# Attention, a dense MoE layer and a routed MoE layer in one program: GpSimd held back at one place, a third PSUM bank for one product, and routing's matmul groups at new places

## The chip, the core and the metric

The program runs on one core of a Trainium2 chip. The core has five engines that run their own instruction streams and wait for one another by semaphores: PE (TensorE, matmuls), DVE (VectorE), ACT (ScalarE), POOL (GpSimd) and SP (SyncE, which here only issues transfers). The metric is the device time of one execution in microseconds; lower is better. A time of this kernel is taken as the median of a few executions, and from one program to the next about 0.2% (1.9 us) can be told from no change.

## What is computed

Three layers follow one another. The tokens are 4 batches of 768, with 8 heads of 64, so x is 3072 x 512 between the layers.

```python
# 1: attention with a window of 128 and 4 sink positions
scores = (q @ k.T) / 8                       # per batch and head
keep   = (pos < 4) | ((0 <= rel) & (rel < 128))
a = softmax(where(keep, scores, -1e9));  x = a @ v
# 2: a dense layer with three input products
h = max(max(x @ w1, x @ w2), x @ w3)         # 512 -> 768
x = h @ w_out                                # 768 -> 512
# 3: routing with a limited capacity, 8 experts of 384 tokens
logits = x @ w_gate
# all (token, expert) pairs are taken in falling order of their logit; a pair is
# skipped if the token is assigned or the expert is full
out[tokens of e] = relu(x[tokens of e] @ w1[e]) @ w2[e]
```

## The kernel before

**Products in three parts.** A matrix product that needs float32 is made from float32r parts: each operand is split into a rounded part (`h`, ACT copies it) and the rest (`l`, a subtraction on DVE or POOL), and PE adds hh, hl and lh. So nearly every tile in the trace has an `h` and an `l`, and for every split there is one ACT instruction and one subtraction.

**Attention** (`class Attn`) works in 32 units: a unit is one batch, one half of the sequence (`hf`) and one pair of heads (`p`); four units make a group, and `n` counts units in the order in which they are loaded. `load` issues the unit's transfers, `prep` splits k (`kh`, the subtraction is L106), q (`qs` by ACT in L107, the rest `ql` in L108) and v (`vsp`, rounded part in L119 on ACT, the rest in L120 on POOL), `score` makes the scores (PE L138, or L140 and L141 for a split unit; tile `ps`) and copies them under the mask into T (`T_w`, `T_x`; in the first units parts of the storage `woh`, `wol` serve as tiles), `soft` does maximum, exponential and sum, with POOL multiplying by the reciprocal (L163), and `pv` transposes T on PE (the sinks' columns into the PSUM tile `pt`, the window's into `pp`, both L25), masks them into A (L179), and multiplies with v (PE L186, L188, L198, L199 into `po`). The first eight units and units 10 and 11 are native: PE takes q, k and v as float32, with no split. **Unit 8 is the first split unit, and unit 9 the second.**

**The dense layer** (`class Moe1`) loads its weights while attention's first units run: `single` puts 64-bit words together to one float32 tile (DVE L245 and L249, ACT L246, POOL L250 into `cA` or a part of `HL`), and `load_w` splits that into `w0`, `w1`, `w2` (ACT L229, POOL L231). There are 18 such words for the input weights, counted by `s.n`, and 6 for w_out. `group` makes the three input products of a group of 384 tokens, 12 matmuls per product (PE L305 into `mm`), and the maximum (ACT L307, DVE L308); it splits the result into `HL`. `x2` multiplies with w_out: 6 products of 18 matmuls each (PE L330), 260 columns wide with the gate's logits in them (n=260) for groups 0 to 4; ACT evicts each (L332, tile `xo`). Group 0 is written out and read back by `reload` (L347 to L350), since its weights are not there in time. Five x2 of this form stand between 175 and 440 us.

**The routed layer** (`class Route`, `class Moe2`). Routing finds one full expert after another: a `phase` counts by digits of the logits, six levels, each with 24 small matmuls (PE L432, tile `rc`), a comparison before it (DVE L427, `th`) and a digit after it (DVE L479 to L483, `met`), then a sum (L490) and ranks (L523, L524, L555). `expert` runs eight blocks f of 12 matmuls (L634) and 9 matmuls (L627), 168 in all, and splits the weights it loads (`wa`, `wb`; ACT L578, DVE L579) and the hidden values (ACT L637, DVE L638). While expert n runs, the routing of expert n+2 runs on DVE, and its groups of small matmuls are put between the expert's matmuls.

**What sets the order.** Attention and the dense layer lie in one block whose instructions a scheduler orders by a timeline of its own when the program is built (`schedule_with_timeline_sim=True`), under priorities, tile pools and the extra dependences that `follow` adds. PSUM has eight banks of 128 x 512 float32: two for `mm`, one each for `pt`, `pp` and `po`, three for `ps`. A pool with one buffer is used strictly in the order in which the program asks for it. Routing's groups are put behind given matmuls of the expert by `behind` and a list of places, one for each group: the six levels, the sum, the two ranks and the slots.

Of the kernel before, what the change touches and what calls it, by code (L numbers as in the profile page):

```python
# [19 lines left out]
FT=mybir.dt.float32; FR=mybir.dt.float32r; BF=mybir.dt.bfloat16; I32=mybir.dt.int32; U8=mybir.dt.uint8; U32=mybir.dt.uint32  # L20
AF=mybir.ActivationFunctionType; OP=mybir.AluOpType; AX=mybir.AxisListType
NEG=-8.0e9
def f32(ap): return ap.bitcast(FT)
# [3 lines left out]
def split(nc,hl,x):  # L27
    i=nc.scalar.activation(hl[0],x,AF.Copy)
    nc.vector.tensor_tensor(hl[1],x,f32(hl[0]),op=OP.subtract)
    return i  # L30

def follow(tc,i,j):
    tc.add_manual_dep(i.ins,j.ins.name,mybir.DependencyInfo(mybir.DependencyClass.NoSync,mybir.DependencyReason.DATA),reason="order on an engine")

class Attn:
    def __init__(s, tc, q,k,v,vs, keep, consts, pst, psp, pss, psv, work):
# [57 lines left out]
    def prep(s,u):  # L94
        nc=s.nc; w=s.w; nb=u['nb']; nat=u['nat']
        half=[(slice(64*h,64*h+64),slice(64-64*h,128-64*h)) for h in range(2)]
        if not nat:
            KK=[s.two(u,[128,4,132],FR,f"kh{h}") for h in range(2)]
            QS=[w.tile([128,384],FR,name=f"qs{h}",bufs=2) for h in range(2)]
            QL=s.ql[u['n']%len(s.ql)]  # L100
            fl=nb*132
            flat=lambda t: t.rearrange("p c j -> p (c j)")[:,:fl]
            for h,(a,o) in enumerate(half):
                k=flat(u['kn'])[a]
                nc.scalar.activation(flat(KK[h])[a],k,AF.Copy)
                nc.vector.tensor_tensor(flat(KK[h])[o],k,f32(flat(KK[h])[a]),op=OP.subtract)  # L106
                nc.scalar.activation(QS[h],u['qn'][h],AF.Copy)  # L107
                nc.vector.tensor_tensor(QL[h][a],u['qn'][h][a],f32(QS[h][a]),op=OP.subtract)  # L108
            u.update(KK=KK,QS=QS,QL=QL)
        VK=u['VK']=s.vk[u['n']%2]  # L110
        hi,lo=(bass.AP(tensor=VK.tensor,offset=VK.offset+o,ap=[[VK.ap[0][0],40],[st,2],[1,64]]) for o,st in (((0,64),(128,64)) if nat else ((0,192),(64,64))))
        nc.gpsimd.tensor_copy(hi,u['sv'])
        nc.gpsimd.tensor_tensor(lo,u['sv'],f32(hi),op=OP.subtract)
        if not nat:

            VS=u['VS']=w.tile([128,4,256],FR,name="vsp")
            hi=bass.AP(tensor=VS.tensor,offset=VS.offset,ap=[list(VS.ap[0]),[256,nb],[192,2],[1,64]])
            lo=bass.AP(tensor=VS.tensor,offset=VS.offset+64,ap=[list(VS.ap[0]),[256,nb],[64,2],[1,64]])
            nc.scalar.activation(hi,u['vn'][:,:nb],AF.Copy)  # L119
            nc.gpsimd.tensor_tensor(lo,u['vn'][:,:nb],f32(hi),op=OP.subtract)  # L120
    def score(s,u):
        nc=s.nc; w=s.w; hf=u['hf']
        if type(s.extra) is not Spare: T=s.two(u,[128,6,132],FT,"T",3)
# [3 lines left out]
        if hf==0:  # L127
            z=nc.gpsimd.memset(T[:,0:2,:],NEG)
            if u['n']==3: follow(s.tc,z,s.ev['s',1])
# [89 lines left out]

class Moe1:  # L220
    def __init__(s, tc, words,wgate, consts, wpool, main, conv, mm, pt, pss, ident):
        s.tc=tc; s.nc=tc.nc; s.mm=mm; s.pss=pss; s.main=main; s.conv=conv; s.ident=ident; s.consts=consts
        s.src=words; s.wgate=wgate
        s.W=[[wpool.tile([128,4,768],FR,name=f"w{i}{x}") for x in "hl"] for i in range(3)]
        s.WO=None; s.at=None; s.stage=None; s.HL=None; s.nx=0; s.second=None; s.n=0; s.loads=[]
        s.WG=main.tile([128,6,16],FR,name="wgt")
    def split(s,src,hi,lo):
        nc=s.nc
        z=nc.scalar.activation(hi,src,AF.Copy)  # L229
        if s.n==5 and s.WO is None: follow(s.tc,z,s.ev['l',4])  # L230
        nc.gpsimd.tensor_tensor(lo,src,f32(hi),op=OP.subtract)  # L231
    def single(s,src,ring=False):

        nc=s.nc
        if ring and s.stage is None: s.stage=s.main.tile([128,12,384],FT,name="HL").rearrange("p a b -> p (a b)").bitcast(I32)
        if ring: st=s.stage[:,s.n%4*1024:(s.n%4+1)*1024].rearrange("p (n t) -> p n t",t=2)
        else: st=s.conv.tile([128,512,2],I32,name="st",bufs=2)
        ld=nc.sync.dma_start(st.rearrange("p n t -> p (n t)"),src.bitcast(I32))
        if ring: s.loads.append(ld)
        else: s.tc.add_manual_dep(ld.ins,s.loads[-6].ins.name,mybir.DependencyInfo(mybir.DependencyClass.NoSync,mybir.DependencyReason.DATA),reason="order of loads")  # L240
        A=(s.mm.tile([128,512],FT,name="mm") if ring and s.n<3 else s.pss.tile([128,512],FT,name="ps")).bitcast(I32); C=st[:,:,0]
        if ring and s.n%3==2: R=s.stage[:,4096:4608]
        else: R=s.conv.tile([128,512],I32,name="cA",bufs=2)
        n=s.n; s.n+=1
        y=nc.vector.tensor_scalar(A,st[:,:,1],0x07ffffff,3,op0=OP.bitwise_and,op1=OP.logical_shift_left)  # L245
        z=nc.scalar.activation(C,st[:,:,0].bitcast(U32),AF.Copy,scale=2.0**-29)  # L246
        if n<4: follow(s.tc,z,s.ev['l',0] if n<2 else s.ev['e',1])
        if n<3: follow(s.tc,y,s.ev['m',1 if n<1 else 2])
        nc.vector.scalar_tensor_tensor(R,st[:,:,1],-0x40000000,A,op0=OP.bitwise_and,op1=OP.bitwise_or)  # L249
        nc.gpsimd.tensor_tensor(R,R,C,op=OP.add)  # L250
        return R.bitcast(FT)
    def pair(s,p):
        return tuple(s.main.tile([128,384],FR,name=f"x{x}{p}",bufs=1) for x in "hl")
# [33 lines left out]
    def group(s,xs,spill=None,pool=None,mid=None,between=None):  # L287
# [3 lines left out]
        for p in range(4):  # L291
            if type(xs[p]) is tuple: X.append(xs[p]); continue
            X.append(s.pair(p))
            with s.tc.high_priority(): split(nc,X[p],xs[p])
# [24 lines left out]
    def x2(s,H,t0,LG,x2d,n=260,pool=None,keep=None):  # L319

        nc=s.nc; main=s.main; mms=[]
        for t in range(3):
            o=pool.tile([128,512],FT,name="xq",bufs=4) if pool else s.room(t).tile([128,520],FT,name="xo",bufs=1)
            for u in range(2):
                c=slice(0,260) if n==260 else slice(4-4*u,260-4*u)
                ps=s.mm.tile([128,512],FT,name="mm")
                k=0
                for f in range(6):
                    for a,b in ((0,0),(0,1),(1,0)):
                        mms.append(nc.tensor.matmul(ps[:,:n],H[f][a][:,t*128:(t+1)*128],s.WO[b][:,f,u,c],start=(k==0),stop=(k==17))); k+=1  # L330
                with s.tc.high_priority():
                    nc.scalar.activation(o[:,u*n:(u+1)*n],ps[:,0:n],AF.Copy)  # L332
                    if keep is not None:
                        for d in (2*u,2*u+1):
                            h,l=keep(t,d); c=ps[:,(d-2*u)*128:(d-2*u)*128+128]
                            nc.scalar.activation(h,c,AF.Copy)
                            nc.vector.tensor_tensor(l,c,f32(h),op=OP.subtract)
            if n==260:
                o,e=s.row(o,0)
                nc.scalar.activation(LG[:,t0+t,:].rearrange("p (u e) -> p u e",u=2),e,AF.Copy)  # L340
            nc.scalar.dma_start(x2d[(t0+t)*128:(t0+t+1)*128,:],o)
        return mms
# [307 lines left out]
def attention_mixtures(tc,q,k,v,vs,words,wg,u1,u2,out,off=60,spread=(0,1,3,4),native=8,order='a0 a0 a0 a0 w a1 w a1 w a1 w a1 w w a2',order1='a2 o o o o o o a2 a2',back=1,at=(1,0),s1=300,s2=400,nring=6):  # L650
    nc=tc.nc
    PS=bass.MemoryType.PSUM
    with ExitStack() as ctx:
        P=lambda n,b,**kw: ctx.enter_context(tc.tile_pool(name=n,bufs=b,**kw))
        A_=lambda n,b,**kw: tc.alloc_tile_pool(name=n,bufs=b,**kw)
        consts=P("consts",1); main=P("main",1); dram=P("dram",1,space=bass.MemoryType.DRAM)
        wpool=A_("wpool",1,side="right"); ac=A_("ac",1); work=A_("work",2); conv=A_("conv",1,side="right")
        mm=P("mm",2,space=PS); pst=P("pst",1,space=PS)
# [62 lines left out]
        E=Moe2(tc,u1,u2,x2d,out,wp,act,main,mm,acc,pst,A.ident,nring,M.part)  # L721
        def step(n):
            e,t=r.phase(n>0) if n<7 else r.last()
            return r.slots(e,t)
        def fet(n):
            G.append([E.fetch(S[n][0],None if n else T7*128),S[n][1],S[n][0]])
        def trn(n):
            G[n][0]=E.turn(G[n][0],None if n else (keep,P7))
            G[n][1]=nc.sync.value_load(G[n][1][0:1,0:1],min_val=0,max_val=7)
        def behind(gs,mms,places):  # L730

            for ins,at in zip(gs,places):
                for i in ins:
                    tc.add_manual_dep(i.ins,mms[at].ins.name,mybir.DependencyInfo(mybir.DependencyClass.NoSync,mybir.DependencyReason.DATA),reason="order on TensorE")
# [22 lines left out]
        for n in range(8):  # L757
            r.groups=[]
            if n<6:
                with tc.high_priority(offset=s2): S.append(step(n+2)); fet(n+2)  # L760
            gs,r.groups=r.groups,[]
            E.expert(*G[n],mid=(lambda: trn(n+1)) if n<7 else None)
            if n<6: behind(gs,E.mms,(40,74,88,102,116,130,143,156,165,167) if n==0 else (20,47,64,81,98,115,131,145,156,160) if n<5 else (4,16))


_INS = ['q', 'k', 'v', 'vs', 'words', 'wg', 'u1', 'u2']
# [50 lines left out]
```

## Time and profile before

| what | us |
|---|---|
| median of three runs (lowest, highest) | 962.07 (961.85, 962.66) |
| the profiled execution, its own time | 963.42 |
| its span, first to last instruction | 961.6 |
| PE busy in the span | 927.3 (96%) |
| DVE busy | 705.2 (73%) |
| ACT busy | 487.7 (51%) |
| POOL busy | 257.1 (27%) |

The profiled execution is 1.35 us above the median, and 1.8 us of its time lie outside its span. Busy time of PE is the time in which a matmul is in flight; matmuls overlap, so a busy PE can still be one that issues below its rate. A wait is the idle time of an engine just before an instruction, and the releaser is the instruction whose end came last. Times in rows count from the span's start.

### The profile page before, as it was taken

The numbers are of one execution on the slowest core, as the hardware profiler recorded it, in microseconds if no ns is written. First come the engines' busy times: TensorE is split into PE (matmuls) and PEld (weight loads), VectorE is DVE, ScalarE is ACT, GpSimd is POOL, SyncE is SP. The second block draws the span as 40 slices with busy tenths as digits, with TensorE's granted clock in tenths as the row PEclk, the third lists the DMA queues.
The fourth block names the chain that finished last, engine by engine and source line by source line (L and its number), as shares of the span: only waits on it lengthen the run. The fifth ranks groups of instructions, "written<-read, shape, count | busy, mean of one in ns | idle before, by whom it ended". The sixth has DMA issues, their size and how long they took to land.

```text
span 961.6 us, 18493 instructions
## 1 busy us (share of the span) xinstructions
PE 927.3 (96%) x6552; PEld 850.4 (88%) x6552; DVE 705.2 (73%) x1867; ACT 487.7 (51%) x1329; POOL 257.1 (27%) x271
## 2 busy tenths in 40 slices
PE   5999899989999999999999999999999999999996
PEld 4688799979999999999999998888888888888895
DVE  7776787687887886778896445888989889874320
ACT  5366474687677675676674211334434434344431
POOL 4676536132321312211231000011103022054321
PEclk9999899999999999999999999999999999999999
DMA  7454321242123121122210002544345353454410
GB/s 233 137 191 144 105 93 64 81 145 68 52 63 94 41 85 57 44 79 85 81 57 1 1 1 88 192 145 132 111 154 176 103 169 119 151 194 156 142 66 33
DMA packets 54443, 99.35 MB, mean 103 GB/s; under 512 B 7792, under 2 KB 24688, under 8 KB 54352
## 3 DMA queue, kind: packets, MB, share of 16 engines
q1 hardware_dynamic: 44464, 75.90, 25.3%
q0 software_dynamic: 3840, 12.45, 3.7%
q10 hardware_dynamic: 6048, 9.83, 2.7%
q8 instruction: 51, 0.84, 0.4%
q14 instruction: 40, 0.33, 0.1%
HBM read 82.17 MB, written 16.12 MB: 102 GB/s over the span
## 4 chain that ended last, share of the span: by engine, by line
PE 82%; DVE 6%; issue 5%; ACT 3%; DMA 2%; POOL 1%; SPq 0%; POOLq 0%; ACTq 0%; DVEq 0%
PE mm L305 28%; PE mm L634 13%; PE acc L627 12%; PE mm L330 8%; PE po L198 3%; PE rc L432 3%; PE po L188 2%; PE pt L25 2%; PE ps L138 2%; PE pp L25 2%; PE ps L140 1%; PE ps L141 1%; PE acc L362 1%; PE po L199 1%; DMA qf<-in_q_dram 1%
## 5 line engine op out<-in xcount | busy, mean ns | idle before, releaser
L627 PE MATMUL acc<-wbh,HL 128*128 128x512 f32 x384 | 133.1, 401 | 0.1
L308 DVE TENSOR_TENSOR hm<-mm,hm 128x384 f32<-128x384 f32 x96 | 53.2, 554 | 50.7 <-PE mm L305 49.5
L330 PE MATMUL mm<-woh,HL 128*128 128x260 f32 (+1 forms) x432 | 86.0, 289 | 2.7 <-ACT xo L332 1.2
L627 PEld LDWEIGHTS acc<-wbh,HL 128*128 128x128 f32 x384 | 71.4, 188 | 12.6 <-ACT HL L637 0.4
L578 ACT ACTIVATE wah<-sa 128x512 fp32r<-128x512 f32 x64 | 40.5, 632 | 82.2 <-PE mm L634 69.3
L578 ACT ACTIVATE wbh<-sb 128x512 fp32r<-128x512 f32 x64 | 40.4, 631 | 72.8 <-PE acc L627 68.9
L627 PE MATMUL acc<-wbl,HL 128*128 128x512 f32 x192 | 76.5, 398 | 0.0
L646 POOL DMA_INDIRECT out_dram<-og,idx x24 | 29.3, 1221 | 168.7 <-ACT og L645 165.9
L330 PEld LDWEIGHTS mm<-woh,HL 128*128 128x128 f32 x432 | 68.4, 188 | 4.7 <-ACT xo L332 1.9
L634 PE MATMUL mm<-HL,wah 128*128 128x384 f32 x256 | 67.5, 341 | 0.0
L305 PE MATMUL mm<-xh,w2h 128*128 128x384 f32 x192 | 66.8, 348 | 0.2 <-ACT hm L307 0.2
L305 PE MATMUL mm<-xh,w1h 128*128 128x384 f32 x192 | 66.1, 344 | 0.8 <-ACT hm L307 0.5
L305 PE MATMUL mm<-xh,w0h 128*128 128x384 f32 x192 | 66.5, 346 | 0.0
L305 PE MATMUL mm<-xl,w0h 128*128 128x384 f32 x192 | 65.4, 341 | 0.0
L305 PE MATMUL mm<-xl,w2h 128*128 128x384 f32 x192 | 65.4, 340 | 0.0
L305 PE MATMUL mm<-xh,w2l 128*128 128x384 f32 x192 | 65.3, 340 | 0.0
L305 PE MATMUL mm<-xh,w1l 128*128 128x384 f32 x192 | 65.3, 340 | 0.0
L579 DVE TENSOR_TENSOR wbl<-sb,wbh 128x512 fp32r<-128x512 f32 x64 | 45.2, 706 | 27.1 <-ACT wbh L578 27.0
L305 PE MATMUL mm<-xh,w0l 128*128 128x384 f32 x192 | 64.9, 338 | 0.0
L305 PE MATMUL mm<-xl,w1h 128*128 128x384 f32 x192 | 64.8, 338 | 0.0
L638 DVE SCALAR_TENSOR_TENSOR HL<-mm,HL 128x384 fp32r<-128x384 f32 x64 | 35.5, 554 | 38.1 <-ACT HL L637 37.8
L163 POOL TENSOR_TENSOR T_w<-T_w,l 128x792 f32<-128x792 f32 x21 | 32.7, 1559 | 108.0 <-DVE l L162 108.0
(334 smaller groups left out, 2815.8 us busy)
## 6 DMA issues: line engine op xcount, KB each, us to landing
sa<-in_u_dram SPq DMA_DIRECT2D x64, 256.0 KB
sb<-in_u_dram SPq DMA_DIRECT2D x64, 256.0 KB
HL<-in_words_dram SPq DMA_DIRECT2D x18, 512.0 KB
qn<-in_q_dram SPq DMA_DIRECT2D x88, 96.0 KB
x2d<-xo ACTq DMA_DIRECT2D x15, 256.0 KB
kn<-in_k_dram SPq DMA_DIRECT2D x12, 264.0 KB
st<-in_words_dram SPq DMA_DIRECT2D x6, 512.0 KB
vn<-in_v_dram SPq DMA_DIRECT2D x12, 256.0 KB
```

What stands on the lines that cost most here:

```text
L25: nc.tensor.transpose(out,x,f32(ident))
L163: s.ev['s',u['n']]=nc.gpsimd.tensor_tensor(T,T,l[:,:,None].to_broadcast([128,6,132]),op=OP.mult)
L198: nc.tensor.matmul(po[:,q:q+n],u['VS'][:,blk,128*h:128*h+128],part[:,c:c+n],start=(part is H and j==0),stop=False,skip_group_check=True)
L305: nc.tensor.matmul(ps[:,:384],s.W[i][a][:,p,f*128:(f+1)*128],X[p][b],start=(n==0),stop=(n==11)); n+=1
L308: else: nc.vector.tensor_tensor(m,ps[:,:384],m,op=OP.max)
L330: mms.append(nc.tensor.matmul(ps[:,:n],H[f][a][:,t*128:(t+1)*128],s.WO[b][:,f,u,c],start=(k==0),stop=(k==17))); k+=1
L578: nc.scalar.activation(h,src,AF.Copy)
L579: (nc.gpsimd if s.n>=6 and nm=="wa" else nc.vector).tensor_tensor(l,src,f32(h),op=OP.subtract)
L627: s.mms.append(nc.tensor.matmul(acc[t],H[f][a][:,t*128:(t+1)*128],W[f][1][b],start=(f==0 and n==0),stop=(f==F-1 and n==2))); n+=1
L634: s.mms.append(nc.tensor.matmul(ps[:,:384],W[f][0][a][:,k,:],X[k][b],start=(n==0),stop=(n==11))); n+=1
L638: nc.vector.scalar_tensor_tensor(l,ps[:,:384],0.0,f32(h),op0=OP.max,op1=OP.subtract)
L646: st=nc.gpsimd.indirect_dma_start(out=s.out,out_offset=bass.IndirectOffsetOnAxis(ap=idx[:,t:t+1],axis=0),in_=o,in_offset=None)
```

## The change

There are three edits, and some renumbering: lines behind L120 stand three lines lower in the changed kernel.

```diff
-def follow(tc,i,j):
-    tc.add_manual_dep(i.ins,j.ins.name,mybir.DependencyInfo(mybir.DependencyClass.NoSync,...
+def follow(tc,i,j,how=mybir.DependencyClass.NoSync):
+    tc.add_manual_dep(i.ins,j.ins.name,mybir.DependencyInfo(how,...
...
 # Attn.prep, the split of q: z is the unit's last subtraction, of the second head
-                nc.vector.tensor_tensor(QL[h][a],u['qn'][h][a],f32(QS[h][a]),op=OP.subtract)
+                z=nc.vector.tensor_tensor(QL[h][a],u['qn'][h][a],f32(QS[h][a]),op=OP.subtract)
...
 # Attn.prep, the split of v
-            nc.gpsimd.tensor_tensor(lo,u['vn'][:,:nb],f32(hi),op=OP.subtract)
+            v=nc.gpsimd.tensor_tensor(lo,u['vn'][:,:nb],f32(hi),op=OP.subtract)
+            if u['n']==8:
+                for x in ('w','c'): follow(s.tc,s.ev[x,16],z,mybir.DependencyClass.Sync)
+            if u['n'] in (8,9): follow(s.tc,v,z,mybir.DependencyClass.Sync)
...
 # Moe1.split and Moe1.single keep their GpSimd instruction
+        s.ev['w',s.n]=nc.gpsimd.tensor_tensor(lo,src,f32(hi),op=OP.subtract)
+        s.ev['c',n]=nc.gpsimd.tensor_tensor(R,R,C,op=OP.add)
...
 # Moe1.x2
-                ps=s.mm.tile([128,512],FT,name="mm")
+                ps=s.pt.tile([128,512],FT,name="pt") if n==260 and (2*t+u)%3==2 else s.mm.tile([128,512],FT,name="mm")
...
 # places of routing's groups, in matmuls of the expert (n<5: of experts 2 to 4 after the change)
-(40,74,88,102,116,130,143,156,165,167) if n==0 else (20,47,64,81,98,115,131,145,156,160) if n<5
+(40,71,92,105,118,131,144,156,165,167) if n==0 else (20,75,85,95,106,117,131,145,156,160) if n==1 else (20,69,79,91,104,117,131,145,156,160) if n<5
```

**The first edit** makes three GpSimd instructions wait for DVE: unit 8's `vsp` (L120), the subtraction of the sixteenth word (`w0l`, L231, `ev['w',16]`) and the addition of the seventeenth (`cA`, L250, `ev['c',16]`) follow unit 8's last `ql`. Unit 9's `vsp` follows unit 9's last `ql`. On POOL, at the place of unit 8 (`w2l` is the fifteenth word's), before:

```order
L231 TENSOR_TENSOR w2l<-HL,w2h 128x4x128
L120 TENSOR_TENSOR vsp<-vn,vsp 128x3x128
L231 TENSOR_TENSOR w0l<-cA,w0h 128x4x128
L250 TENSOR_TENSOR cA<-cA,HL 128x512
L250 TENSOR_TENSOR HL<-HL 128x512
L231 TENSOR_TENSOR w1l<-cA,w1h 128x4x128
```

and of the change, from the same `w2l` on:

```order
L234 TENSOR_TENSOR w2l<-HL,w2h 128x4x128
L234 TENSOR_TENSOR w0l<-cA,w0h 128x4x128
L253 TENSOR_TENSOR cA<-cA,HL 128x512
L120 TENSOR_TENSOR vsp<-vn,vsp 128x3x128
L253 TENSOR_TENSOR HL<-HL 128x512
L234 TENSOR_TENSOR w1l<-cA,w1h 128x4x128
```

`vsp` has moved behind `w0l` and `cA`, and all three now stand behind a wait for DVE. PE's and DVE's orders are the same in both kernels up to here.

**The second edit** gives the third and the sixth of x2's six products the bank of `pt`, which until now held the sinks' transposes alone; the scheduler then puts attention and the dense layer in another order from the first x2 to the end of the block. On PE, at the first x2, before (T_w and T_x are softmax tiles of two units, each L330 one matmul of 260 columns, 18 of them in a row at the first "..."):

```order
L25 MATMUL pt<-ident,T_w 128x128 x3
L25 MATMUL pp<-ident,T_w 128x128 x3
...
L330 MATMUL mm<-woh,HL 128x260
L330 MATMUL mm<-wol,HL 128x260
...
L25 MATMUL pp<-ident,T_w 128x128 x3
L186 MATMUL po<-psb_105,vk_103 128x384 x2
...
L25 MATMUL pt<-ident,T_x 128x128 x3
```

and of the change:

```order
L25 MATMUL pt<-ident,T_w 128x128 x3
L25 MATMUL pp<-ident,T_w 128x128 x3
L143 MATMUL ps<-kh_w,qs_2359 128x260
L144 MATMUL ps<-kh_w,ql_111 128x260
L25 MATMUL pp<-ident,T_w 128x128 x3
...
L25 MATMUL pt<-ident,T_x 128x128 x3
...
L333 MATMUL pt<-woh,HL 128x260
L333 MATMUL pt<-wol,HL 128x260
```

Before, 30 of x2's matmuls stood between T_w's and T_x's transposes; of the change none does, and the first product into `pt` comes behind T_x's last transpose.

**The third edit** moves groups of small matmuls. For experts 2 to 4 the levels after the first stood after 61, 70, 82, 99 and 116 of the expert's 168 matmuls and now stand after 70, 80, 92, 105 and 118; the first level (37) and the sum (132) stay. For expert 1 they stood after 70, 78, 88, 99 and 116 and now after 76, 87, 98, 108 and 119, for expert 0 after 75, 89, 103, 117 and 131 and now after 73, 93, 106, 119 and 132. On DVE, in expert 2 between the second level's comparison and its digit, before:

```order
L427 TENSOR_TENSOR th<-z,thr 128x24x64
L475 SCALAR_TENSOR_TENSOR w<-z,digs 128x24
L579 TENSOR_TENSOR wbl<-sb,wbh 128x512
L479 TENSOR_SCALAR met,digit_9773<-rc,roomp 128x63
L480 STREAM_TRANSPOSE digits<-digit_9773 128x32
```

and of the change:

```order
L430 TENSOR_TENSOR th<-z,thr 128x24x64
L478 SCALAR_TENSOR_TENSOR w<-z,digs 128x24
L582 TENSOR_TENSOR wbl<-sb,wbh 128x512
L582 TENSOR_TENSOR wal<-sa,wah 128x512
L641 SCALAR_TENSOR_TENSOR HL<-mm,HL 128x384
L482 TENSOR_SCALAR met,digit_9773<-rc,roomp 128x63
```

Two more instructions stand ahead of the digit, and as many fewer follow between later levels.

## Rows read from the trace of the kernel before

**Rows 1.** The page's busy time: us, share of the span, instructions.

```profile
PE 927.3 (96%) x6552; PEld 850.4 (88%) x6552; DVE 705.2 (73%) x1867; ACT 487.7 (51%) x1329; POOL 257.1 (27%) x271
```

**Rows 2.** PE's waits over the span: releaser, us in total, times, longest.

```profile
PE ps L140 <- DVE kh_w L106: 4.6, 1, 4.6
...
PE ps L140 <- DVE T_x L150: 1.4, 1, 1.4
...
PE mm L330 <- ACT xo L332: 1.2, 2, 1.0
```

**Rows 3.** Windows, experts 0 to 4: us, busy of PE, PEld, DVE, ACT, POOL, clock.

```profile
640.00:860.00 220.00, 219.91 (x1912) 191.62 (x1911) 199.64 (x728) 88.66 (x166) 41.12 (x33) 1.00 0.42 138
```

**Rows 4.** Timeline around unit 8's scores: start, us, instruction, count, idle before.

```profile
98.85 1.28 POOL L231 TENSOR_TENSOR w2l<-HL,w2h 128x512 fp32r<-128x512 f32 x1
...
99.32 5.25 DVE L106 TENSOR_TENSOR kh_w<-kn,kh_w 64x396 fp32r<-64x396 f32 x2 [1.14 <-ACT kh_w L105]
...
100.10 0.98 POOL L120 TENSOR_TENSOR vsp<-vn,vsp 128x384 fp32r<-128x384 f32 x1
101.05 1.25 POOL L231 TENSOR_TENSOR w0l<-cA,w0h 128x512 fp32r<-128x512 f32 x1
102.27 1.26 POOL L250 TENSOR_TENSOR cA<-cA,HL 128x512 int32<-128x512 int32 x1
...
104.59 1.14 DVE L108 TENSOR_TENSOR ql<-qn,qs 64x384 fp32r<-64x384 f32 x2
...
106.19 0.63 PE L305 MATMUL mm<-xh,w2l 128*128 128x384 f32 x1
...
109.35 0.28 PE L140 MATMUL ps<-kh_w,qs 128*128 128x260 f32 x1
...
109.59 0.34 PE L305 MATMUL mm<-xh,w0h 128*128 128x384 f32 x1
109.76 0.34 PE L305 MATMUL mm<-xl,w0h 128*128 128x384 f32 x1
```

**Rows 5.** Line L106 over the span: duration in ns, least/median/most.

```profile
L106 DVE TENSOR_TENSOR kh_w<-kn,kh_w x24: 564/702/4648, 99.3 to 460.0; 64x396 fp32r<-64x396 f32 x12, 64x528 fp32r<-64x528 f32 x12
```

**Rows 6.** Windows, the same columns, then DMA share and GB/s.

```profile
20.40:27.20 6.80, 5.88 (x18) 4.05 (x19) 6.07 (x16) 4.82 (x19) 5.20 (x7) 0.50 0.48 135
...
104.10:109.10 5.00, 4.99 (x19) 5.00 (x20) 4.77 (x11) 0.48 (x1) 1.29 (x1) 0.50 0.47 126
...
195.00:216.00 21.00, 17.87 (x118) 14.37 (x117) 19.16 (x38) 17.21 (x62) 8.20 (x8) 1.00 0.49 151
```

**Rows 7.** Timeline around another blocked L106, DVE and POOL.

```profile
317.80 1.29 POOL L120 TENSOR_TENSOR vsp<-vn,vsp 128x512 fp32r<-128x512 f32 x1 [0.21 <-ACT vsp L119]
317.81 1.84 DVE L106 TENSOR_TENSOR kh_w<-kn,kh_w 64x528 fp32r<-64x528 f32 x1
319.05 0.93 POOL L113 TENSOR_TENSOR vk<-vns,vk 40x128 fp32r<-40x128 f32 x1
```

**Rows 8.** Timeline of what follows unit 8's scores: ACT, POOL, PE.

```profile
110.43 0.94 ACT L107 ACTIVATE qs<-qn 128x384 fp32r<-128x384 f32 x2 [4.69 <-DMA qn<-in_q_dram]
...
111.97 1.28 POOL L231 TENSOR_TENSOR w1l<-cA,w1h 128x512 fp32r<-128x512 f32 x1 [4.14 <-ACT w1h L229]
...
115.06 0.34 PE L305 MATMUL mm<-xh,w1l 128*128 128x384 f32 x1
```

**Rows 9.** Windows of L330 alone at the first x2: us, PE busy (count), PEld busy.

```profile
191.10:199.50 8.40, 4.19 (x30) 3.79 (x30) 1.00 0.56 175
```

**Rows 10.** Timeline of expert 2 at its closest pair of levels: PE and DVE.

```profile
740.21 0.87 PE L432 MATMUL rc<-th,ohr 128*128 128x64 bf16 x24
741.13 0.28 DVE L479 TENSOR_SCALAR_CACHE_REDUCE met<-rc,roomp 128x63 bf16<-128x63 f32 x1 [0.29 <-PE rc L432]
...
742.21 0.56 DVE L427 TENSOR_TENSOR th<-z,thr 128x768 bf16<-128x768 bf16 x1
...
742.83 0.76 PE L432 MATMUL rc<-th,ohr 128*128 128x32 bf16 x24
```

More of the change, by code (lines that the diff above doesn't have):

```diff
@@ L30, in split @@
     return i
-def follow(tc,i,j):
-    tc.add_manual_dep(i.ins,j.ins.name,mybir.DependencyInfo(mybir.DependencyClass.NoSync,mybir.DependencyReason.DATA),reason="order on an engine")
+def follow(tc,i,j,how=mybir.DependencyClass.NoSync):
+    tc.add_manual_dep(i.ins,j.ins.name,mybir.DependencyInfo(how,mybir.DependencyReason.DATA),reason="order on an engine")
 class Attn:
@@ L221, in __init__ @@
     def __init__(s, tc, words,wgate, consts, wpool, main, conv, mm, pt, pss, ident):
-        s.tc=tc; s.nc=tc.nc; s.mm=mm; s.pss=pss; s.main=main; s.conv=conv; s.ident=ident; s.consts=consts
+        s.tc=tc; s.nc=tc.nc; s.mm=mm; s.pss=pss; s.pt=pt; s.main=main; s.conv=conv; s.ident=ident; s.consts=consts
         s.src=words; s.wgate=wgate
@@ L230, in split @@
         if s.n==5 and s.WO is None: follow(s.tc,z,s.ev['l',4])
-        nc.gpsimd.tensor_tensor(lo,src,f32(hi),op=OP.subtract)
+        s.ev['w',s.n]=nc.gpsimd.tensor_tensor(lo,src,f32(hi),op=OP.subtract)
     def single(s,src,ring=False):
@@ L249, in single @@
         nc.vector.scalar_tensor_tensor(R,st[:,:,1],-0x40000000,A,op0=OP.bitwise_and,op1=OP.bitwise_or)
-        nc.gpsimd.tensor_tensor(R,R,C,op=OP.add)
+        s.ev['c',n]=nc.gpsimd.tensor_tensor(R,R,C,op=OP.add)
         return R.bitcast(FT)
@@ L762, in attention_mixtures @@
             E.expert(*G[n],mid=(lambda: trn(n+1)) if n<7 else None)
-            if n<6: behind(gs,E.mms,(40,74,88,102,116,130,143,156,165,167) if n==0 else (20,47,64,81,98,115,131,145,156,160) if n<5 else (4,16))
+            if n<6: behind(gs,E.mms,(40,71,92,105,118,131,144,156,165,167) if n==0 else (20,75,85,95,106,117,131,145,156,160) if n==1 else (20,69,79,91,104,117,131,145,156,160) if n<5 else (4,16))
 _INS = ['q', 'k', 'v', 'vs', 'words', 'wg', 'u1', 'u2']
```

## The prediction

> **What bounds the kernel now.** The page's busy time comes first: PE works in 927.3 of 961.6 us, and no other engine passes 73% [rows 1]. So an edit can gain only where PE stands still, or where it runs at the lower of its clocks. PE's waits, added up by releaser, show where it stands still: one wait of 4.6 us for `kh_w` of L106, then single waits of 1 us or so, all of them in the stretch where x2 and the last attention units share the engines [rows 2]. The windows of the routed layer show the contrary: from 640 to 860 us PE is busy for 219.91 of 220 us, and DVE, next, for 199.64 [rows 3]. The timeline around the longest wait then shows its cause. Unit 8's first L106 on DVE starts at 99.32, and the longest of that line's 24 instructions takes 4.648 us where the median is 0.702 [rows 4, 5]: it ends at 103.97. In these 4.65 us POOL runs four instructions without a gap: `w2l` from 98.85 to 100.13, `vsp` to 101.08, `w0l` to 102.30 and `cA` to 103.53 [rows 4]. DVE's instruction ends 0.44 us behind the last of them. It did not run slowly beside POOL; it stood until POOL was through.
>
> A second cost hangs on this wait. In the 5 us behind it the granted clock is 0.50, the lower of the two levels, 1.2 GHz [rows 6]. The ten L305 between 106.19 and 109.35 take 3.16 us, while a step from one to the next is 0.17 us once the clock is back (109.59 to 109.76) [rows 4]; ten such steps are 1.7 us.
>
> **The first edit.** In the changed kernel `w2l` still meets L106, but behind it POOL must wait for the second L108. I take L106 as free at `w2l`'s end, 100.13. How it ends then is seen at 317.81, where an L106 met `vsp` at 317.80 and ended at 319.65, 0.56 us behind `vsp`'s end [rows 7]. That gives 100.69 here. The second L106 took 0.60 us (5.25 for both less 4.65) and the two L108 1.14 us [rows 4], so the last `ql` is there at 100.69 + 0.60 + 1.14 = 102.43. Before, it was there at 104.59 + 1.14 = 105.73. PE's next product began 0.46 us behind that, at 106.19. **The product starts 3.3 us earlier.** PE's stall shrinks from 4.6 to about 1.3 us. In the first x2 PE has idle 21.00 - 17.87 = 3.1 us, with a wait of 1.4 us among it, and the granted clock stays 1.00 there [rows 2, 6], so I let it stay up here as well: 3.16 - 1.7 = 1.46 us more. **Together -4.7.** The bounds: if the clock falls in spite of the shorter stall, a stretch of half clock like that from 20.4 to 27.2, 6.8 us long [rows 6], costs up to half of it, 3.4 us, less the 0.4 or so of it that PE spends waiting: the gain sinks to -1.7. If DVE were let in before `w2l` ends, 0.8 us more come out: -5.5.
>
> What the three held instructions cost is hidden, I think. POOL is free until 102.43, then `w0l` ends at 103.7, `cA` at 104.9, `vsp` at 105.9. The first product that needs `w0l` comes two steps behind 109.59, moved by 4.7 to 105.2: 1.5 us of cover. POOL's next addition (`HL`) waits for DVE's own instruction on that word in both kernels. The closest is `w1l`: unit 9's `qs` on ACT waits for a transfer until 110.43, `w1l` ran from 111.97 to 113.25, and PE wanted it at 115.06, 1.8 us later [rows 8]. The transfer is issued behind the second L108, so it moves by 3.3, PE's need by 4.7, and the other `w1h` order on ACT gives back 0.2 or so: a margin of 0.6 us is left. If it is used up, PE waits for the difference, some tenths. Unit 9's `vsp` waits for a unit whose DVE work PE needs first anyway; nothing.
>
> The Trainium skill says in "SBUF — State Buffer", section "Who interferes with whom", that a DVE instruction with two SBUF inputs contends with a GpSimd instruction that reads SBUF, and that whichever has the lock fully blocks the other until its instruction finishes. Read strictly, DVE would get in when `w2l` ends, as at 317.81 [rows 7], and holding the other three back would be worth nothing; by the row, L106 stood until `cA` was through [rows 4], and the edit is worth 4.7. The row decides, with a rival below for the other reading.
>
> **The second edit.** What it can win are waits in the x2 stretch. Those on ACT's eviction `xo`, 1.2 us in two [rows 2], are waits for a bank: a third bank gives the product somewhere to go. The 3.1 us idle in the first x2 [rows 6] are on DVE's softmax and splits; DVE is busy for 19.16 of those 21 us, so a bank does nothing for it, though the new order might. What it can lose stands at the same place. Before, 30 matmuls of x2, 4.19 us of PE time, stood between 191.1 and 199.5 [rows 9], between `T_w`'s and `T_x`'s transposes; in the changed order none does, and PE may come to `T_x` 4.2 us before DVE. On the other hand the product of x2 is not lost: it comes later and can fill a later hole. Only what is not refilled is a loss. The bounds are a gain of 3.1 + 1.2 = 4.3 and a loss of 4.2 + 3.4 (a half clock behind it, as above) = 7.6. **I take -1.2**, because the bank explains that wait and the filler moved to where the 3.1 us lie.
>
> **The third edit.** Each group needs DVE's comparison ahead of it and a digit behind it; a group placed too close makes PE wait. The closest pair of before lies in expert 2: the digit follows at 741.13, the next comparison is ready at 742.77 and PE takes it at 742.83 [rows 10], 9 matmuls apart. After the change the least distance is 10. PE does not wait in this stretch now [rows 3], so larger distances win nothing. DVE's other work in between (`wal`, `HL`) comes at other places, and PE waits if an `HL` is late; a level's margin is of the order of the 0.06 us between 742.77 and 742.83 [rows 10], so a shift of an instruction such as the 0.28 us digit either way is the size of a miss: 5 experts by 0.3 is 1.5. **I take 0, with 1.5 either way.**
>
> **The sum.** -4.7 - 1.2 + 0 = -5.9. The profiled execution took 963.42, so 957.5 is what it would take; it lies 1.35 above the median of the runs shown, 962.07, and **I predict 956.2 for the median**. What this kernel's measurement can tell from no change is 0.2%, 1.9 us.
>
> **Rivals.** *The clock falls all the same*: the shorter stall is still followed by a half clock. For it speaks that the clock fell around 20.4 in a stretch where PE was busy for 5.88 of 6.8 us [rows 6], against it the first x2. Then -1.7 - 1.2 = -2.9: 959.2. *The new order finds more*: the waits on DVE in the x2 stretch go too, about 3.4 us besides the 1.2: 952.8. For it speaks that x2's matmuls move to other gaps, against it that DVE is nearly full there. *The first x2 lacks its filler*: 4.2 us lost less half refilled, or all of it with the clock down, so that 956.2 becomes 958.5 to 963; middle 960.5. For it speaks that T_x stood 1.4 us late even with the filler [rows 2]. *The hold changes nothing*: the lock passes to DVE at every instruction's end, and L106 was slow for another reason (a transfer, its own 64 x 396 shape). Then only the second edit's 1.2 is left: 960.9. Against it speak the second L106 at 0.60 us and the end 0.44 us behind `cA` [rows 4]. *Slower than before*: the sinks' bank becomes the bound. Ten products of five x2 now stand in `pt`'s queue, and each holds the bank for its 18 matmuls and its eviction; the transposes of the sinks wait behind it, and with them the softmax output that PV needs. 18 matmuls at 4.19 / 30 = 0.14 are 2.5 us [rows 9]. If in each x2 a transpose comes too early and PE waits 1.6 us for it, that is 8 us, more than the 5.9 + 1.9 at which it decides: 964 and above. Against it speaks that in the changed order `pt`'s product stands behind the last transpose at the first x2.
>
> **How the numbers follow.** My sum 0.45 (its own range, from the smaller terms' errors of about 2 us: 954.3 to 958.4); the clock falls 0.14; more found 0.13; no filler 0.13; the hold does nothing 0.07; slower 0.08. The range from 952.3 to 961.5 leaves out the slower case and the far ends of the cases "more found" and "no filler", together less than 0.2. Faster by over 1.9 us, below 960.15: the sum, the falling clock's upper three quarters, more found, half of the lacking filler, a little of the idle hold: 0.45 + 0.11 + 0.13 + 0.07 + 0.01 = 0.77. Slower, above 964: 0.08 with little of the fourth case. The rest, 0.15, within 0.2%.
>
> **What would show it.** Right: L106 ends near 100.7, the wait at unit 8 is 1.3 us or less, the granted clock from 101 to 107 is 1.00 and the next product starts near 102.9; no wait for `w0l`, `w1l` or unit 8's `vsp`; no PE wait for `xo`; from 640 to 860 still no wait. Wrong: an L106 of over 3 us at this place though POOL stands; a half clock behind it; waits at `T_x`, `pt` or L333 of over 3 us between 180 and 440; a wait at L435 for `th`, or at L630 for `HL`, in the experts.

## The result, and the profile after

The changed kernel is slower: median 968.70 us of 16 runs, against 962.59 us of 16 runs of the kernel before beside them; ratio 1.0059 (95% interval 1.0048 to 1.0071). The profiled execution took 970.82 us, its span is 969.1 us, 7.5 more than before. The prediction was 956.2, in a range from 952.3 to 961.5.

The page's busy time of the changed kernel stands against [rows 1]. The same 6552 matmuls keep PE busy for 4.2 us longer, so some of them ran slower; the other 3.3 of the 7.5 us are time in which PE stands idle.

```profile
PE 931.5 (96%) x6552; PEld 852.9 (88%) x6552; DVE 708.3 (73%) x1867; ACT 489.1 (50%) x1329; POOL 260.3 (27%) x271
```

PE's waits in the changed kernel by releaser (us in total, times, longest), against [rows 2]:

```profile
PE ps L141 <- DMA qf<-in_q_dram: 9.1, 3, 4.9
PE mm L308 <- DVE hm L311: 3.3, 1, 3.3
PE pp L25 <- DVE A_w L182: 2.9, 2, 2.6
PE mm L333 <- DVE HL L353: 2.1, 3, 1.3
...
PE mm L333 <- ACT HL L352: 1.6, 1, 1.6
PE ps L143 <- DVE kh_w L106: 1.2, 1, 1.2
```

The first edit did what was worked out: the wait for `kh_w` fell from 4.6 to 1.2 us. The first row lies in the first 23 us of the program, where the profiles of kernels with the same order differ too (the kernel before has 4.8 us for `wol` and 2.8 for `qf` there). Three waits are new or have grown: for `hm` (3.3), for `A_w` (2.9; 0.5 before), and for `HL` of `reload`, 3.7 in two rows where the kernel before has 1.1.

The timeline around unit 8's scores, DVE, POOL and PE in turn, against [rows 4]:

```profile
100.33 1.86 DVE L106 TENSOR_TENSOR kh_w<-kn,kh_w 64x396 fp32r<-64x396 f32 x2 [1.13 <-ACT kh_w L105]
102.22 1.14 DVE L108 TENSOR_TENSOR ql<-qn,qs 64x384 fp32r<-64x384 f32 x2
...
99.89 1.28 POOL L234 TENSOR_TENSOR w2l<-HL,w2h 128x512 fp32r<-128x512 f32 x1
103.44 1.28 POOL L234 TENSOR_TENSOR w0l<-cA,w0h 128x512 fp32r<-128x512 f32 x1 [2.27 <-DVE ql L108]
...
101.73 0.30 PE L143 MATMUL ps<-kh_w,qs 128*128 128x132 f32 x1 [1.22 <-DVE kh_w L106]
...
103.68 0.63 PE L308 MATMUL mm<-xh,w2l 128*128 128x384 f32 x1
...
106.89 0.28 PE L143 MATMUL ps<-kh_w,qs 128*128 128x260 f32 x1
```

From the start of L106 to PE's product it is 103.68 - 100.33 = 3.35 us, before 106.19 - 99.32 = 6.87: 3.5 us won. The ten L308 still take 106.89 - 103.68 = 3.21 us, at half the clock.

The loss is read from windows (us, busy of PE, PEld, DVE, ACT and POOL with counts, clock, DMA share, GB/s) of the changed kernel over the first x2 and what follows it, then of its part at half clock, then around the wait for `hm`:

```profile
184.10:229.30 45.20, 37.68 (x242) 31.42 (x241) 37.76 (x65) 33.79 (x120) 11.57 (x11) 0.92 0.35 106
...
189.50:195.50 6.00, 5.78 (x20) 4.23 (x21) 5.33 (x11) 3.28 (x15) 2.52 (x3) 0.50 0.21 61
...
484.50:499.00 14.50, 11.16 (x62) 10.12 (x61) 12.94 (x20) 9.64 (x31) 3.95 (x4) 0.89 0.25 82
```

and of the kernel before over the same counts of PE's matmuls:

```profile
186.60:223.10 36.50, 33.37 (x242) 29.43 (x242) 31.64 (x62) 30.46 (x107) 10.96 (x10) 1.00 0.39 120
...
480.70:490.40 9.70, 9.70 (x62) 9.04 (x61) 9.60 (x18) 7.64 (x24) 4.40 (x4) 1.00 0.25 72
```

**The first x2 and what follows it cost 45.2 - 36.5 = 8.7 us.** PE is idle for 7.5 us instead of 3.1, and the same 242 matmuls keep it busy for 4.3 us longer; about 3 of these are the 6.0 us at half clock. PE's waits in this stretch of the kernel before are

```profile
PE ps L140 <- DVE T_x L150: 1.4, 1, 1.4
PE mm L330 <- DVE HL L350: 0.8, 1, 0.8
PE ps L140 <- DVE T_w L150: 0.5, 1, 0.5
PE mm L330 <- ACT HL L349: 0.3, 1, 0.3
```

and all four lie between 202.6 and 212.8 us, behind the first x2, whose last matmul begins at 193.24.

**The stretch around `hm` costs 14.5 - 9.7 = 4.8 us.** Counted at the same number of PE's matmuls in both traces, the new order wins 2.4 back between the two and 1.1 behind the second, and PE was 1.1 later in this execution before unit 8. With the 3.5 won at unit 8: 8.7 - 2.4 + 4.8 - 1.1 - 3.5 + 1.1 = 7.6, the span's 7.5.

PE's timeline at the first x2 of the changed kernel shows the hole:

```profile
185.75 0.49 PE L25 MATMUL pt<-ident,T_w 128*128 128x128 f32 x3
...
186.88 0.28 PE L144 MATMUL ps<-kh_w,ql 128*128 128x260 f32 x1
189.72 0.90 PE L25 MATMUL pp<-ident,T_w 128*128 128x128 f32 x3 [2.56 <-DVE A_w L182]
...
195.71 0.49 PE L25 MATMUL pt<-ident,T_x 128*128 128x128 f32 x3
...
202.42 0.39 PE L333 MATMUL pt<-woh,HL 128*128 128x260 f32 x1
```

PE stands from 187 to 189.7 with nothing to issue. The two products for `pt`, 36 matmuls, read the same `HL` and weights as the four for `mm`, and those had begun all their 72 matmuls by 185.08; so the operands of the 36 are there. But they stand behind `T_x`'s transposes and begin at 202.42. In the kernel before 30 of x2's matmuls stand between `T_w`'s and `T_x`'s transposes [rows 9]: the last 18 of the first x2, and 12 of `reload`'s. Another 18 of the displaced 36 had stood ahead of `T_w`'s transposes (90 before them, now 72), so PE also came to these about 2 us sooner.

And the wait for `hm`, in DVE's and POOL's rows:

```profile
491.13 4.25 DVE L29 TENSOR_TENSOR xl<-x,xh 128x384 fp32r<-128x384 f32 x3
495.30 0.54 DVE L311 TENSOR_TENSOR hm<-mm,hm 128x384 f32<-128x384 f32 x1
...
491.29 1.72 POOL L166 TENSOR_TENSOR T_x<-T_x,l 128x792 f32<-128x792 f32 x1 [1.60 <-DVE l L165]
492.98 0.76 POOL L113 TENSOR_TENSOR vk<-vns,vk 40x128 fp32r<-40x128 f32 x1
493.70 1.25 POOL L120 TENSOR_TENSOR vsp<-vn,vsp 128x512 fp32r<-128x512 f32 x1
```

Here three POOL instructions run without a gap, and three DVE subtractions of 0.55 us take 4.25 together. It resembles unit 8, but is not the same: the second subtraction ended at 493.43, 0.42 us behind `T_x`'s end and while `vk` ran, so DVE got in between two POOL instructions; the third then stood until 495.37, 0.42 behind the end of `vsp`. The first edit took such a meeting away; the new order made another.

### The profile page after: what moved, and what is told of

It is laid out like the page before. It is cut to its first block, busy times and chain, and to the rows that moved or that the text cites. A ratio compares the mean times of both kernels' runs of the same rounds, so it can differ in the third digit from the quotient of the medians.

```text
span 969.1 us, 18491 instructions
## 1 busy us (share of the span) xinstructions
PE 931.5 (96%) x6552; PEld 852.9 (88%) x6552; DVE 708.3 (73%) x1867; ACT 489.1 (50%) x1329; POOL 260.3 (27%) x271
## 4 chain that ended last, share of the span: by engine, by line
PE 83%; DVE 5%; issue 4%; ACT 3%; DMA 3%; POOL 1%; SPq 0%; POOLq 0%; ACTq 0%; DVEq 0%
PE mm L308 30%; PE acc L630 12%; PE mm L637 12%; PE mm L333 6%; PE po L201 3%; PE rc L435 3%; PE po L191 3%; PE pt L25 2%; PE pp L25 2%; PE pt L333 2%; PE ps L141 2%; PE ps L143 1%; PE ps L144 1%; DMA HL<-in_words_dram 1%; PE acc L365 1%
## 5 line engine op out<-in xcount | busy, mean ns | idle before, releaser
L308 PE MATMUL mm<-xh,w0h 128*128 128x384 f32 x192 | 66.9, 348 | 3.3 <-DVE hm L311 3.3
L308 PE MATMUL mm<-xh,w2h 128*128 128x384 f32 x192 | 66.6, 347 | 0.3 <-ACT hm L310 0.3
L308 PE MATMUL mm<-xh,w1h 128*128 128x384 f32 x192 | 66.1, 344 | 0.8 <-ACT hm L310 0.5
L333 PE MATMUL mm<-woh,HL 128*128 128x260 f32 (+1 forms) x312 | 62.5, 290 | 4.2 <-DVE HL L353 2.1
L308 PE MATMUL mm<-xl,w0h 128*128 128x384 f32 x192 | 66.4, 346 | 0.0
L308 PE MATMUL mm<-xh,w2l 128*128 128x384 f32 x192 | 65.8, 343 | 0.0
L308 PE MATMUL mm<-xh,w0l 128*128 128x384 f32 x192 | 65.7, 342 | 0.0
L308 PE MATMUL mm<-xl,w2h 128*128 128x384 f32 x192 | 65.7, 342 | 0.0
L308 PE MATMUL mm<-xh,w1l 128*128 128x384 f32 x192 | 65.6, 341 | 0.0
L308 PE MATMUL mm<-xl,w1h 128*128 128x384 f32 x192 | 65.4, 340 | 0.0
L182 DVE TENSOR_TENSOR A_w<-pp,ul 128x768 f32<-128x768 f32 x54 | 51.2, 949 | 6.3 <-PE pp L25 4.8
```

The costliest lines, as they stand in the source:

```text
L182: nc.vector.tensor_tensor(A,pt[:,:384].rearrange("p (i q) -> p i q",q=128)[:,:,None,:].to_broadcast([128,3,2,128]), s.ul[:,None,:,:].to_br ...
L308: nc.tensor.matmul(ps[:,:384],s.W[i][a][:,p,f*128:(f+1)*128],X[p][b],start=(n==0),stop=(n==11)); n+=1
```

## The experiments

Theory 1: the hold and the places are worth what the prediction said, and the third bank makes the loss, because two of the first x2's products wait in the queue of the sinks' bank. Rivals: the hold's gain is lost later (2), any third bank leads to such an order (3), the places cost (4). In e2 the number 3 stands for another rival, that hold and bank make the loss together, and in e5 and e6 the number 2 for the later x2 and the meeting at 491 as its source. The "before" beside each ratio is the kernel before on the same chip. First and third edit together (e4) are called the base.

| run | median | before | ratio (95%) |
|---|---|---|---|
| e1, hold alone | 959.88 | 962.88 | 0.9964 (0.9944 to 0.9984) |
| e2, bank alone | 972.89 | 962.88 | 1.0096 (1.0070 to 1.0122) |
| e3, places alone | 962.90 | 962.88 | 1.0004 (0.9984 to 1.0024) |
| e4, hold and places | 958.02 | 962.88 | 0.9948 (0.9928 to 0.9968) |
| e5, base, bank in the first x2 only | 974.04 | 963.28 | 1.0112 (1.0094 to 1.0130) |
| e6, base, bank in all but the first x2 | 958.38 | 963.28 | 0.9943 (0.9928 to 0.9958) |
| e7, base, third bank from the scores | 964.38 | 963.28 | 1.0008 (0.9996 to 1.0019) |
| e8, changed kernel, unit 29's POOL held | 966.53 | 963.28 | 1.0036 (1.0021 to 1.0050) |
| e9, hold of the words alone | 969.34 | 971.57 | 0.9963 (0.9939 to 0.9987) |
| e10, hold of `vsp` alone | 971.03 | 971.57 | 0.9985 (0.9960 to 1.0009) |
| e11, base, bank in the last three x2 | 961.77 | 971.57 | 0.9878 (0.9841 to 0.9916) |
| e12, places alone, again | 965.99 | 972.03 | 0.9943 (0.9920 to 0.9965) |

**e1 to e4: each edit by itself.** e1 is the kernel before with the first part of the diff, e2 with the line in `x2`, e3 with the line of places; e4 is the changed kernel with this undone:

```diff
-                ps=s.pt.tile([128,512],FT,name="pt") if n==260 and (2*t+u)%3==2 else s.mm.tile([128,512],FT,name="mm")
+                ps=s.mm.tile([128,512],FT,name="mm")
```

e1: 

> The kernel before with the first edit alone (GpSimd's three instructions and unit 9's vsp behind VectorE); PE's and DVE's orders are those of before. Theory 1 (the hold gives what the trace of the changed kernel shows behind unit 8, the loss comes from the third bank): the wait for kh_w is 1.2 us instead of 4.6, half a clock still follows, and the time falls by 3.5 us, ratio 0.9964. Theory 2 (the hold pushes GpSimd's work into a later stretch, so that its gain is lost again): the wait shrinks too, but the time is within 1 us of before, ratio 0.999 to 1.001.

e2: 

> The kernel before with the second edit alone (the third and sixth product of x2 in the sinks' bank). Theory 1: all of the loss is here: +9 us in the first x2 and some us of waits and gains behind it, in all +9 to +10, ratio 1.010, and PE waits 2.6 us for A_w near 192. Theory 2: the bank costs only about what the whole change costs, +6, ratio 1.006. Theory 3 (the collisions come from the hold and the bank together): +4 or less.

e3: 

> The kernel before with the third edit alone (other places of routing's groups in experts 0 to 4). Theory 1: no change, ratio 0.999 to 1.001, and PE busy for all but 0.2 us of 640 to 860. Theory 4 (the places cost part of the loss): +1.5 us or more, ratio above 1.0015, with waits of PE for th or HL.

e4: 

> The changed kernel with the second edit undone (first and third edit). Theory 1: as the first edit alone, -3.5 us, ratio 0.9964. Theory 2: within 1 us of before. Theory 4: -2 or less.

All four ratios fit theory 1 within their intervals, with one miss: in e1 no half clock followed (below). The three ratios multiply to 1.0064, the whole change has 1.0059. In e2 the two new waits stand there without the hold:

```profile
PE pp L25 <- DVE A_w L179: 3.2, 3, 2.6
PE mm L305 <- DVE hm L308: 3.2, 1, 3.2
```

In e1 PE's stall is the same 1.2 us as in the changed kernel, but the granted clock stays at 1.00 behind it, where it is 0.59 from 103 to 105 us in the changed kernel. DVE's and PE's timeline of e1:

```profile
97.76 1.85 DVE L106 TENSOR_TENSOR kh_w<-kn,kh_w 64x396 fp32r<-64x396 f32 x2 [1.01 <-ACT kh_w L105]
...
99.16 0.30 PE L143 MATMUL ps<-kh_w,qs 128*128 128x132 f32 x1 [1.23 <-DVE kh_w L106]
...
101.00 0.39 PE L308 MATMUL mm<-xh,w2l 128*128 128x384 f32 x1
...
102.81 0.28 PE L143 MATMUL ps<-kh_w,qs 128*128 128x260 f32 x1
```

The ten L308 take 102.81 - 101.00 = 1.81 us here, and 3.21 in the changed kernel. From the start of L106 to the end of the ten it is 102.81 - 97.76 = 5.05 us in e1, 106.89 - 100.33 = 6.56 in the changed kernel and 109.35 - 99.32 = 10.03 before [rows 4]: 5.0 us won in the one, 3.5 in the other.

**e5 to e7: where the bank hurts, and whether it is the bank.** Each is the base with another condition, or another pool:

```diff
+ # e5
+                ps=s.pt.tile(...) if n==260 and t0==3 and (2*t+u)%3==2 else s.mm.tile(...)
+ # e6
+                ps=s.pt.tile(...) if n==260 and t0!=3 and (2*t+u)%3==2 else s.mm.tile(...)
+ # e7
+                ps=s.pss.tile([128,512],FT,name="ps") if n==260 and (2*t+u)%3==2 else s.mm.tile(...)
```

e5: 

> The changed kernel, but only the first x2 (of the second group) has products in the sinks' bank; the other four have two banks as before. Theory 1 (the loss is made at the first x2: its two products in pt wait in that bank's queue behind T_x's transposes, so that the 36 matmuls are missing in the hole): +8 to +9 us against first and third edit alone, which is a ratio to before of 1.003 to 1.0045, and PE waits about 2.6 us for A_w near 190. Theory 2 (the later x2 and the collision at 491 make the loss, the first x2's products only move): within 2 us of first and third edit alone, ratio 0.994 to 0.997.

e6: 

> The changed kernel with the first x2 taken back to two banks; the other four keep the third. Theory 1: the wait for A_w is gone, and the time is within 2 us of first and third edit alone, ratio 0.993 to 0.997. Theory 2: most of the loss stays, ratio 1.002 to 1.006.

e7: 

> The changed kernel with the third and sixth product in one of the scores' three banks instead of the sinks' one. Theory 1 (the sinks' queue is the cause, not the third bank): filler stands between T_w's and T_x's transposes, no wait for A_w of over 1 us near 190, ratio below 0.999 unless the scores now lack a bank (then PE waits for T_w or T_x at the scores). Theory 3 (any third bank leads the scheduler to such an order): the wait for A_w stays, ratio 1.003 or more.

e5 and e6 decide between theories 1 and 2: with the bank in the first x2 alone the whole loss is there, without it none. PE's longest waits from 175 to 250 us, in e5 and in e6:

```profile
PE pp L25 <- DVE A_w L182: 2.9, 2, 2.6
PE mm L333 <- ACT HL L352: 2.4, 1, 2.4
```

```profile
PE mm L333 <- DVE HL L353: 0.8, 1, 0.8
```

In size theory 1 was too low: e5 is 1.6% or 16 us above e4, not 8 to 9. It has further waits behind the first x2, of which the largest are for `reload`'s `HL` (2.4) and, near 300, for `HL` of the next group (1.8), each with half a clock behind it: counted at the same number of PE's matmuls in e5 and e4, 12 us are lost up to 231 in e5 and 6 more between 275 and 307. PE's order in e5 leaves the changed kernel's at 209.5, so its 16 us are not the first x2's share of the changed kernel's loss. e7 speaks against theory 3 at the first x2: from 175 to 250 us the profile shows no wait of PE. But it is not fast, and its 1.0008 fits neither forecast (below 0.999, or 1.003 and more). Between 440 and 540 us PE waits 9.3 us in it, 2.0 for `HL`, 1.6 in four for `x`, 1.5 each for `hm` and `T_w`. So with another bank the loss at the first x2 is gone, and a loss of about 6 us against e4 (1.0008 and 0.9948) stands elsewhere; why it comes out there was not taken apart.

**e8: the second meeting.** In the changed kernel unit 29's `vk` and `vsp` wait for the third of the three `xl`; the order on every engine is the same:

```diff
+            if u['n']==29:
+                for i in (y,v): follow(s.tc,i,s.ev['xl',6,2],mybir.DependencyClass.Sync)
```

(`y` is the subtraction of L113, `s.ev['xl',6,2]` the third `xl` of the seventh group.) 

> The changed kernel, with unit 29's vk and vsp on GpSimd made to wait for VectorE's third xl of the seventh group; the order on every engine is that of the changed kernel. If GpSimd's run of three holds VectorE at 491, as the four did at 99: the third xl ends 1.4 us earlier (only the first of the three, T_x times l, still meets VectorE), PE's wait of 3.3 us for hm falls to 1.9, and with the clock up behind it the time falls by 1.4 to 2.6, ratio 1.003 to 1.0045. If VectorE's xl is slow for another reason: the wait stays 3.3 and the ratio 1.006.

PE's wait and DVE's and POOL's rows in e8:

```profile
PE mm L310 <- DVE hm L313: 1.7, 1, 1.7
```

```profile
488.88 2.77 DVE L29 TENSOR_TENSOR xl<-x,xh 128x384 fp32r<-128x384 f32 x3
...
489.05 1.72 POOL L168 TENSOR_TENSOR T_x<-T_x,l 128x792 f32<-128x792 f32 x1 [1.44 <-DVE l L167]
491.80 0.45 POOL L113 TENSOR_TENSOR vk<-vns,vk 40x128 fp32r<-40x128 f32 x1 [1.03 <-DVE xl L29]
```

The three take 4.25 - 2.77 = 1.5 us less, and the wait, 3.3 before, is 1.7. In the two profiles PE's matmuls behind this stretch come 3.0 us sooner in e8, counted from those ahead of it: 1.6 of the wait, and the half clock behind it, which e8 does not have. The ratio falls from 1.0059 to 1.0036, about 2.2 us, but the two intervals (1.0048 to 1.0071, 1.0021 to 1.0050) overlap a little. So by the profiles 3.0 of the 4.8 us hang on this meeting.

**e9 and e10: the dose of the hold.** The kernel before with only a part of the first edit:

```diff
+ # e9
+            if u['n']==8:
+                for x in ('w','c'): follow(s.tc,s.ev[x,16],z,mybir.DependencyClass.Sync)
+ # e10
+            if u['n']==8: follow(s.tc,v,z,mybir.DependencyClass.Sync)
```

e9: 

> The kernel before with only w0l and cA held behind VectorE; unit 8's vsp and unit 9's are free, and the order on every engine is that of before. If each GpSimd instruction of the run holds L106 for as long as it lasts: L106 ends 0.4 to 0.6 us behind vsp's end, 1 us later than with all three held, PE's wait for kh_w is 2.2 us (4.6 before, 1.2 with all three), and the time falls by 2.4 us with half a clock behind it, ratio 0.9975, or 3.8 without, 0.996. If VectorE gets in between two GpSimd instructions: the wait is 1.2.

e10: 

> The kernel before with only unit 8's vsp held; GpSimd runs w2l, w0l and cA without a gap. If the run of instructions holds L106: it ends behind cA, 1 us earlier than before (vsp's 0.98), PE's wait is 3.6 us, the clock falls as before, and the ratio is 0.999. If VectorE gets in between two: the wait is 1.2 and the ratio 0.9965 or less.

PE's waits at unit 8 in e9 and in e10:

```profile
PE ps L142 <- DVE kh_w L106: 2.2, 1, 2.2
```

```profile
PE ps L141 <- DVE kh_w L106: 3.6, 1, 3.6
```

With one, two, three and four POOL instructions in the run the wait is 1.2, 2.2, 3.6 and 4.6 us: each adds its own time (`vsp` 1.0, `w0l` and `cA` 2.4). The waits decide, the times do not: e10's interval holds 1, and e9's holds both of its forecasts, 0.9975 with a half clock behind the wait (which its profile has) and 0.996 without.

**e11 and e12: the late x2, and the places on other chips.** e11 is the base with `n==260 and t0>3` in the condition; e12 is e3 again.

e11: 

> First and third edit, and the third bank only in the last three of the five x2. If the bank is worth its xo waits there (1.2 us in two), the ratio is 0.993 to 0.994, 0.5 to 1.2 us under first and third edit alone; if its products only move other work, the same as these, 0.995, or above.

e12: 

> The third edit alone, once more. In the last three runs ScalarE and VectorE started some instructions of the routed layer up to 3.8 us late, behind no instruction that the profile shows; PE then waited for th, 6.9 us in five with the places of before and 2.2 us in five with the new places. If that lateness is there again, the third edit alone is worth about 4.7 us, ratio 0.995, and the kernel before takes about 971. If it is not there, before takes about 963 and the ratio is 1.000 as in the first run of this edit.

e9 to e12 ran on two chips on which the kernel before takes 971.6 and 972.0 us, and on the second of them, in e12, the third edit is worth 0.57%, where e3 on another chip found nothing (1.0004). PE's waits for `th` in the routed layer with the places of before (e9), and with the new ones (e12):

```profile
PE rc L434 <- DVE th L429: 6.9, 5, 2.3
```

```profile
PE rc L432 <- DVE th L427: 2.6, 6, 1.0
```

e11's 0.9878 therefore holds the third edit's 0.57% and the hold's 0.36%; what is left, 0.3%, is inside its interval, and whether the bank is worth anything in the last three x2 stays open.

## Why the prediction was wrong, step by step

**The first edit: right.** 3.3 us were worked out for the earlier product, 3.5 came. The clock was taken to stay up, with its fall as a rival; both happened, at the same stall of 1.2 us: in the changed kernel and e11 the clock fell, in e1 and e4 to e8 it did not. The 1.46 us for it was the right size (3.21 - 1.81 = 1.40), so of the term's 4.7 us 5.0 came at unit 8 in e1's profile and 3.5 in the changed kernel's; e1's median gives 3.5, with an interval from 1.5 to 5.4. What decides between the two was not found. The cover was right too: no wait for `w0l`, `w1l` or unit 8's `vsp`. The Trainium skill says in "SBUF — State Buffer", section "Who interferes with whom", that the port pair which DVE shares with GpSimd is an exclusive lock. The prediction's strict reading of it, that DVE gets in when one GpSimd instruction ends, would have given 1.2 us of wait in e9 and e10 as well; at unit 8 the trace does not agree with that reading, the waits were 2.2 and 3.6 us.

**The third edit: right on e3's chip** (1.0004), and worth 5.5 us on e12's. The prediction's 0.06 us of margin at the second level was read as the size of a miss. That a place without a margin turns any lateness of ACT or DVE into a wait of PE would fit the 6.9 us for `th` in e9 and the 2.6 in e12, but no run tests it.

**The second edit: this step failed.** It was put as "-1.2, because the bank explains that wait and the filler moved to where the 3.1 us lie"; by itself it costs 9.2 us (1.0096, with an interval from 6.7 to 11.7 us), where the prediction's bound was a loss of 7.6. The waits for `xo` that it reasoned from did go away: the changed kernel has none at L333. Three things were wrong in it. First, it had seen that no x2 matmul stands between `T_w`'s and `T_x`'s transposes, and treated the 30 displaced ones as a filler that only changes its hole. But the 3.1 us idle of before lie behind the first x2, not in it, and come when DVE is behind; where the filler had stood PE ran ahead of DVE, stood for 2.6 us and went on at half clock for 6 us. The filler was also undercounted: besides the 30, 18 more had stood ahead of `T_w`'s transposes. Second, when the displaced products came, from 202 on, they were followed at once by those of `reload`, whose `HL` were not there: 3.7 us of waits, 2.6 more than before. Third, an order that changes over 280 us brings new meetings of POOL and DVE; the stretch around one of them, at 491, cost 4.8 us, of which e8 gives back 3.0. The rival "the first x2 lacks its filler" named the place, the idle time and the half clock, with a chance of 0.13 and half of it refilled; at the first x2 nothing was, and 2.4 us came back later. Its amounts were low: 4.2 + 3.4 us on top of 956.2 is 963.8, not 963, and without the -1.2 that it contradicts it is 965.0 (962.07 - 4.7 + 7.6), outside the range that was given. For it the prediction named `T_x`'s 1.4 us [rows 2]; that row is a product of the scores at 212.72, behind the filler, and `T_x`'s transposes at 199.53 did not wait. The rival on the slower side, `pt`'s queue, named the bank but the wrong victim: not the transposes wait for the products, the products wait for the transposes.

One reading of rows was incomplete: among PE's waits before there are also 4.8 us for `wol`, 2.8 for `qf` and 2.1 for `wol` in the first 23 us, so not all others are single waits of 1 us in the stretch of x2. None of the edits touches them.

## What to carry to other kernels

A second use of a buffer that is taken strictly in order queues ready work behind the first use: look at what stands next to a long wait of another engine, and ask whether the work that used to hide it can still be issued there. When an edit makes a scheduler reorder hundreds of instructions, its own term is the small one; look in the new order for holes without filler and for runs of GpSimd instructions beside VectorE, and forecast with a range that reaches to the other sign. The first edit of this change helps, the third helped on one chip of two, and the second hurts at one place: without the bank in the first x2, 0.9943 (e6), and without it at all, 0.9948 (e4), beat both the kernel before and the changed one. Between these two no difference is shown, so the third bank has not been shown to win anything anywhere.

## What the runs showed of the hardware

- At unit 8 a run of GpSimd instructions without a gap held a VectorE instruction until its end (1.2, 2.2, 3.6, 4.6 us of wait for one to four). That is not the common case: of six VectorE subtractions of the kernel before that lost over 0.4 us to a GpSimd instruction with another right behind it, four were through within 0.6 to 0.8 us of the first one's end, while the next ran (at 210.77, at 317.81 [rows 7], at 494.52 and at 507.37), and two stood through a further one (at 99.32, and at 262.40). What decides that was not found.
- The same stall of 1.2 us at the same place was followed by half a clock in two of the eight profiled runs with the whole hold; 1.4 us hang on it. Behind the stall of 4.6 us the clock fell in all four profiled runs without the hold (before, e2, e3 and e12).
- On two chips engines started instructions of the routed layer late without a releaser that the profile names. In e9 ACT's longest such wait is this row of its waits from 640 to 860 us:

```profile
ACT wah L580 <- remote: 3.8, 1, 3.8
```

  Durations of the instructions themselves were those of the other chips (on average `wal` 683 ns in e9 and 684 before, `th` 689 in both). The cause is open.
